# A gated-MLP block behind a long convolution: right-angle transform in four channel units, first half ordered by a list scheduler inside the kernel

## The chip, the cores and the metric

One core of one Trainium2 chip runs the kernel. The metric is the device time of one launch in microseconds (us), lower is better.

## The reference, cut to what matters

All tensors are bf16; S = 2048 rows, D = 640 channels, Fh = 864.

```python
mod = silu(c) @ w_mod                      # six vectors of 640: sa, ca, ga, sb, cb, gb
h = layernorm(x) * (1 + ca) + sa           # x = A_q
kv = conv4(A_k, shift_k) * A_v             # 4 causal taps per channel
y = irfft(rfft(kv, 2S) * rfft(ssm_k, 2S))[:S] + kv * ssm_D
x = x + ga * (h * y)
h = layernorm(x) * (1 + cb) + sb
z = gelu(h @ w_in)                         # 2048 x 1728
z1 = z[:, :864]; z2 = layernorm(z[:, 864:])
out = x + gb * ((z1 * (w_sp @ z2 + b_sp)) @ w_out)
```

The first half is everything up to the second `x`; the second half is the gated MLP.

## The kernel before, in words

**Inputs and tables of the first half.** A_k and A_v are loaded transposed (channels on partitions) by ten transposing DMAs on SP's queue (L140, L141). TensorE applies the four taps as matmuls with diagonal weights `dg` (L165), VectorE multiplies by v (L167), and the product goes to a DRAM scratch `kv_scr` (L168), from which it is read back as `XU` in the layout of the transform (L501). The transform is two steps of matmuls: step one multiplies by a cos/sin table `F1bd` (helper at L263, copied out of PSUM by ScalarE at L222 into `X1K` or `X1U`), step two by the table `M2`. M2 is made from iota, range reduction on VectorE (L181 to L189) and Sin on ScalarE (L185 to L190). `G2`, its transpose for the way back, is made by 51 TensorE transposes (L304).

**Row statistics and modulation.** The whole of x is normalised on VectorE (L356, L357) and ScalarE (L363), with a square root on ScalarE (L84). Six matrices `wm` of w_mod are loaded through two buffers and multiplied on TensorE (L380, L389), giving `gca_bf` and `gsa_bf`; GpSimd applies these to the gate `gh` (L495).

**The main loop** runs over four units of 160 channels and, in each, over 17 blocks of 128 frequencies (`kc`); blocks 0 and 16 are real, the other 15 complex. For one block of the data side TensorE forms `pu` (L244 to L252, four matmuls of 160 columns), VectorE multiplies by the kernel's transform `KH` (L416, tile `T`, 640 elements), TensorE goes back (L424, L428, eight matmuls of 160 columns into `pz`) and ScalarE copies to `Z` (L222). In the same loop TensorE and ScalarE make `KH` of the next unit (`pk`), step one of the next unit, and the way back of the unit before: TensorE transposes Z (L449, tile `pt`), VectorE copies it (L224, tile `ZT`), TensorE multiplies by `Ebd` (L459, tile `py`), and VectorE multiplies the gate (L463). Once a unit is done VectorE adds it to x (L467) and takes the statistics of the new x (L474). The third slot of KH is filled by a DMA (L286).

**The second half**: statistics and normalisation (L567, L577), TensorE transposes and their copies into `h2T` (L582, L586, L588), then four dense products on TensorE: z2 (L605), z1 (L621), w_sp times z2 (L642), and the output (L658). `w_in` (L552), `w_o` (L555) and the transposed w_sp, `wT` (L562), are loaded when the buffers of the first half are free; GpSimd multiplies w_o by gb (L557).

**What sets the order.** The kernel is written in the Tile framework: pools give buffers, semaphores follow from the tiles, and the framework's own scheduler may move instructions. Inside the main loop the author interleaves the lists of a unit by hand (`interleave`).

Of the kernel before, what the change touches and what calls it, by code (L numbers as in the profile page):

```python
# [10 lines left out]
ALU = mybir.AluOpType  # L11
# [26 lines left out]
def kernel(  # L38
# [39 lines left out]

    constp = ctx.enter_context(tc.tile_pool(name="constp", bufs=1))
# [14 lines left out]
    eps_t = constp.tile([P, 1], F32)  # L94
    nc.vector.memset(eps_t[:], EPS)
# [5 lines left out]
    ones_row = constp.tile([1, P], BF16)  # L101
    nc.vector.memset(ones_row[:], 1.0)
    zeros_bf = constp.tile([P, DU], BF16)
    nc.vector.memset(zeros_bf[:], 0.0)

    with ExitStack() as actx:
# [7 lines left out]
        gsa_bf = consta.tile([P, D], BF16)  # L114
        sk_bf = consta.tile([P, ND, 4], BF16)
        c_bf = consta.tile([P, ND], BF16)

        kpool = actx.enter_context(tc.tile_pool(name="kside", bufs=2))
        psA = actx.enter_context(tc.tile_pool(name="psA", bufs=2, space=bass.MemoryType.PSUM))
        ectx = ExitStack()  # L120
        early = ectx.enter_context(tc.tile_pool(name="early", bufs=2))
        psE = ectx.enter_context(tc.tile_pool(name="psE", bufs=2, space=bass.MemoryType.PSUM))

        nc.sync.dma_start(sk_bf[:], A_shift_k.rearrange("(t p) j -> p t j", p=P))
        ssm_fft = A_ssm_k.rearrange("(c g) (n f) -> (g n) c f", g=8, f=P)
        XK0 = kpool.tile([P, NCU, P], BF16, tag="XK")
        nc.sync.dma_start(XK0[:], ssm_fft[:, 0:NCU, :])
        d_fft = A_ssm_D.rearrange("(c g) -> g c", g=8)

        def add_D(XK, c0):  # L130
            nc.gpsimd.dma_start(out=XK[0:P:16, :, 0], in_=d_fft[:, c0:c0 + NCU], accum_op=ALU.add)

        add_D(XK0, 0)
        nc.sync.dma_start(c_bf[:], c[0].rearrange("(t p) -> p t", p=P))
        kv_in = []
        for dt in range(ND):
            kTp = early.tile([P, KPAD + S], BF16, tag="kTp", bufs=ND)
            vT = early.tile([P, S], BF16, tag="vT", bufs=ND)
            nc.gpsimd.memset(kTp[:, 0:KPAD], 0.0)
            nc.sync.dma_start_transpose(kTp[:, KPAD:], A_k[0, :, dt * P:(dt + 1) * P])  # L140
            nc.sync.dma_start_transpose(vT[:], A_v[0, :, dt * P:(dt + 1) * P])  # L141
            kv_in.append((kTp, vT))
        nc.sync.dma_start(xt[:], x_nat)
        wmv = w_mod.rearrange("(t p) (j d) -> p t j d", p=P, j=6)
        wm_tiles = []
        for j in range(6):
            wm = consta.tile([P, ND, D], BF16, tag="wm", bufs=2)
            nc.sync.dma_start(wm[:], wmv[:, :, j, :])
            wm_tiles.append(wm)

        sk = early.tile([P, ND, 4], F32, bufs=1)
        dg = early.tile([P, ND, 4, P], BF16, bufs=1)
        nc.vector.tensor_copy(sk[:], sk_bf[:])
        for dt in range(ND):
            nc.vector.tensor_tensor(dg[:, dt], ident[:, None, :].to_broadcast([P, 4, P]),
                                    sk[:, dt, :, None].to_broadcast([P, 4, P]), op=ALU.mult)
        kv_scr = dram.tile([D, S], BF16)
        SCH = 512
        for dt in range(ND):
            kTp, vT = kv_in[dt]  # L160
            for sc_i in range(S // SCH):
                ps = psE.tile([P, SCH], F32, tag="kv")
                for j in range(4):
                    o = KPAD + sc_i * SCH - j
                    nc.tensor.matmul(ps[:], lhsT=dg[:, dt, j, :], rhs=kTp[:, o:o + SCH], start=(j == 0), stop=(j == 3))  # L165
                vsl = vT[:, sc_i * SCH:(sc_i + 1) * SCH]
                nc.vector.tensor_tensor(vsl, ps[:], vsl, op=ALU.mult)  # L167
            nc.sync.dma_start(kv_scr[dt * P:(dt + 1) * P, :], vT[:])  # L168
        if "kv" in dbg:
            nc.sync.dma_start(dbg["kv"], kv_scr[:])  # L170

        cctx = ExitStack()
        cs = cctx.enter_context(tc.tile_pool(name="cscratch", bufs=2))
        TWO_PI = float(np.float32(2 * np.pi * (1 - 2.0 ** -20)))
        MAGIC = 12582912.0
        halfpi = consta.tile([P, 1], F32)
        nc.vector.memset(halfpi[:], float(np.float32(np.pi / 2 * (1 - 2.0 ** -20))))

        def sincos(dst_cos, dst_nsin, dst_sin, v, shape, tagp):
            r = cs.tile(shape, F32, tag=tagp + "r")  # L180
            nc.vector.tensor_scalar(r[:], v, MAGIC, MAGIC, op0=ALU.add, op1=ALU.subtract)  # L181
            fr = cs.tile(shape, F32, tag=tagp + "fr")
            nc.vector.tensor_tensor(fr[:], v, r[:], op=ALU.subtract)
            if dst_nsin is not None:
                nc.scalar.activation(dst_nsin, fr[:], ACT.Sin, scale=-TWO_PI)  # L185
            if dst_sin is not None:
                nc.scalar.activation(dst_sin, fr[:], ACT.Sin, scale=TWO_PI)
            if dst_cos is not None:
                nc.vector.scalar_tensor_tensor(r[:], fr[:], -1.0, fr[:], op0=ALU.mult, op1=ALU.max)  # L189
                nc.scalar.activation(dst_cos, r[:], ACT.Sin, bias=halfpi[:], scale=-TWO_PI)  # L190

        pq = cs.tile([P, 1], F32, bufs=1)
# [499 lines left out]
```

## Time and profile before

| | us |
|---|---|
| device time, median of 3 runs | 449.6 |
| lowest and highest run | 447.17, 450.35 |
| span of the profiled execution, first to last instruction | 446.3 |
| TensorE busy in it | 361.0 |
| VectorE busy | 238.1 |
| ScalarE busy | 177.2 |
| GpSimd busy | 64.5 |

The profiled execution has its span only, no time of its own; the span is 3.3 us under the median of the runs. PE is TensorE's matrix multiply, PEld its weight load, DVE VectorE, ACT ScalarE, POOL GpSimd, SPq SyncE's queue of DMA issues. A duration in the trace runs from the start to the end of one instruction; instructions of one engine that follow each other overlap a little, so the interval between two starts is shorter than the duration.

### The profile page before, as it was taken

What the parts mean: (1) busy time and instruction counts of PE and PEld (TensorE: products, weight loads), DVE (VectorE), ACT (ScalarE), POOL (GpSimd) and SP (SyncE); (2) the same over time, 40 slices, a digit from 0 to 9 for tenths busy, and PEclk for the clock granted to TensorE, in tenths of its full rate; (3) what the DMA queues carried; (4) which work ended last, traced back from release to release, by engine and by line L of the source; (5) the groups of instructions that cost most, each with busy time, mean ns of one, the idle gap of its engine ahead of it and who ended that gap; (6) DMA issues with size and microseconds to landing.
All of it is one profiled execution on the core that took longest, in us unless ns stands there. A gap on an engine that the chain in (4) does not pass through costs nothing.

```text
span 446.3 us, 6827 instructions
## 1 busy us (share of the span) xinstructions
PE 361.0 (81%) x2777; PEld 230.8 (52%) x2777; DVE 238.1 (53%) x526; ACT 177.2 (40%) x356; POOL 64.5 (14%) x68
## 2 busy tenths in 40 slices
PE   1975643684979989979552789999999999999996
PEld 0333631362967868868341455444444444445774
DVE  4779900140447777879769887640132333233553
ACT  1338888455866867823201655765200000000000
POOL 2001000799920000000100710000000000000000
PEclk9997865687999999999855799999999999999999
DMA  8999891720250050020109999500000000000222
GB/s 149 203 227 391 268 208 16 220 60 7 54 123 1 2 123 1 1 65 1 24 3 301 239 214 199 101 1 0 1 0 13 0 12 1 0 1 0 74 89 74
DMA packets 96991, 38.73 MB, mean 87 GB/s; under 512 B 86752, under 2 KB 95552, under 8 KB 96960
## 3 DMA queue, kind: packets, MB, share of 16 engines
q1 hardware_dynamic: 95424, 37.77, 34.3%
q0 software_dynamic: 1536, 0.53, 1.0%
q8 instruction: 21, 0.34, 0.3%
q14 instruction: 10, 0.08, 0.1%
HBM read 16.63 MB, written 5.24 MB: 49 GB/s over the span
## 4 chain that ended last, share of the span: by engine, by line
PE 46%; DVE 7%; DMA 2%; SPq 1%; issue 1%; ACT 0%; DVEq 0%
PE ps L642 22%; PE ps L658 7%; PE ps L621 7%; PE ps L605 6%; DMA w_in<-in_B_w_in_dram 2%; DVE T L416 2%; DVE xn L577 1%; PE pt L449 1%; DVE ZT L224 1%; PE pz L424 1%; PE py L459 1%; SPq L562 1%; DVE st L474 1%; PE pz L428 1%; PE pt L582 1%
## 5 line engine op out<-in xcount | busy, mean ns | idle before, releaser
L642 PE MATMUL ps<-wT,z 128*128 128x512 bf16 (+1 forms) x448 | 96.9, 379 | 0.0
L642 PEld LDWEIGHTS <-z 128*128 128x128 bf16 (+1 forms) x448 | 45.4, 101 | 51.3
L416 DVE TENSOR_TENSOR T<-pu,KH 128x640 bf16<-128x640 f32 x68 | 53.7, 815 | 32.4 <-PE pu L252 23.2
L645 DVE TENSOR_TENSOR gt<-ps,bsp_bc 128x512 bf16<-128x512 f32 (+1 forms) x28 | 19.3, 691 | 85.0 <-PE ps L642 85.0
L222 ACT CAST Z<-pz 128x320 bf16<-128x320 f32 x64 | 27.3, 426 | 32.5 <-PE pz L428 25.8
L424 PE MATMUL pz<-T,G 128*128 128x160 bf16 x272 | 30.4, 234 | 6.8 <-DVE T L416 6.4
L605 PE MATMUL ps<-w_in,h2T 128*128 128x432 bf16 x160 | 31.9, 351 | 0.8 <-DMA w_in<-in_B_w_in_dram 0.8
L165 PE MATMUL ps<-kTp,dg 128*128 128x512 bf16 x80 | 21.7, 413 | 13.4 <-DMA kTp<-in_A_k_dram 9.7
L638 POOL DMA_DIRECT2D bsp_bc<-in_B_b_sp_dram x4 | 2.3, 589 | 200.5 <-DVE gt L645 106.3
L658 PE MATMUL ps<-w_o,z1T 128*128 128x320 bf16 (+1 forms) x224 | 30.7, 299 | 0.0
L621 PE MATMUL ps<-h2T,w_in 128*128 128x512 bf16 (+1 forms) x140 | 30.4, 379 | 0.0
L222 ACT CAST X1K<-ps 128x512 bf16<-128x512 f32 x40 | 23.4, 586 | 14.8 <-PE ps L263 14.1
L222 ACT CAST KH<-pk 128x320 bf16<-128x320 f32 x68 | 26.9, 440 | 1.8 <-PE pk L252 0.9
L428 PE MATMUL pz<-T,G 128*128 128x160 bf16 x240 | 27.2, 234 | 0.0
L424 PEld LDWEIGHTS <-G 128*128 128x128 bf16 x272 | 20.7, 98 | 11.9 <-DVE T L416 7.0
L658 PEld LDWEIGHTS <-z1T 128*128 128x128 bf16 (+1 forms) x224 | 21.8, 97 | 8.9
L263 PE MATMUL ps<-F1bd,XU 128*128 128x256 bf16 x80 | 17.9, 300 | 8.6 <-ACT X1U L222 4.8
L495 POOL TENSOR_TENSOR gh<-gh,gca_bf 128x640 bf16<-128x640 bf16 x16 | 22.4, 1422 | 10.3 <-DVE gca_bf L393 10.3
L660 DVE TENSOR_TENSOR ot<-ps,xt 128x320 bf16<-128x320 f32 x32 | 15.7, 491 | 14.2 <-PE ps L658 14.2
L621 PEld LDWEIGHTS <-w_in 128*128 128x128 bf16 (+1 forms) x140 | 14.2, 102 | 16.0 <-issue 0.2
L611 DVE BATCH_NORM_STATS2 stz<-z 128x6 f32<-128x432 bf16 x32 | 19.4, 608 | 5.1 <-ACT z L608 4.3
L495 POOL TENSOR_TENSOR gh<-gh,gsa_bf 128x640 bf16<-128x640 bf16 x16 | 21.9, 1390 | 0.0
(132 smaller groups left out, 616.8 us busy)
## 6 DMA issues: line engine op xcount, KB each, us to landing
wm<-in_w_mod_dram SPq DMA_DIRECT2D x6, 800.0 KB, 5.4
KH<-KH SPq DMA_DIRECT2D x4, 680.0 KB, 5.5
xt<-in_A_q_dram SPq DMA_DIRECT2D x1, 2560.0 KB, 10.9
kv_scr<-vT SPq DMA_DIRECT2D x5, 512.0 KB, 10.6
XU<-kv_scr SPq DMA_DIRECT2D x4, 640.0 KB, 5.6
out_dram<-ot SPq DMA_DIRECT2D x16, 160.0 KB, 1.8
w_in<-in_B_w_in_dram SPq DMA_DIRECT2D x1, 2160.0 KB, 10.8
XKn<-in_A_ssm_k_dram SPq DMA_DIRECT2D x3, 640.0 KB, 7.7
```

The lines of the kernel that those rows point to most:

```text
L165: nc.tensor.matmul(ps[:], lhsT=dg[:, dt, j, :], rhs=kTp[:, o:o + SCH], start=(j == 0), stop=(j == 3))
L222: nc.scalar.copy(dst, src)
L416: nc.vector.tensor_tensor(T[:], pu[:, None, :, :].to_broadcast([P, 2, 2, DU]), kx, op=ALU.mult)
L424: nc.tensor.matmul(zre, lhsT=w_, rhs=x_, start=(i == 0), stop=(i == 3))
L428: nc.tensor.matmul(pz[:, 1, :], lhsT=w_, rhs=x_, start=(i == 0), stop=(i == 3))
L495: nc.gpsimd.tensor_tensor(gvu, gvu, vec[:, None, d0:d0 + DU].to_broadcast([P, GHB, DU]), op=op)
L605: nc.tensor.matmul(ps[:, :FC], lhsT=h2T[:, kt, n * P:(n + 1) * P], rhs=w_in[:, kt, Fh + fc * FC:Fh + (fc + 1) * FC], start=(kt == 0), stop ...
L611: nc.vector.bn_stats(out=stz[:, n, fc * nsubz + a, :], in_=zs[:, a, :])
L621: nc.tensor.matmul(ps[:fsz[ft], :], lhsT=w_in[:, kt, ft * P:ft * P + fsz[ft]], rhs=h2T[:, kt, sc_i * SC:(sc_i + 1) * SC], start=(kt == 0), ...
L642: nc.tensor.matmul(ps[:fsz[ft], :], lhsT=z2[:, st_i, ft * P:ft * P + fsz[ft]], rhs=wT[:, st_i, tci * TC:(tci + 1) * TC], start=(st_i == 0) ...
L645: nc.vector.tensor_tensor(gt[:fsz[ft], :], ps[:fsz[ft], :], bsp_bc[:fsz[ft], :], op=ALU.add)
L658: nc.tensor.matmul(ps[:, :HS], lhsT=z1T[:fsz[ft], ft, n * P:(n + 1) * P], rhs=w_o[:fsz[ft], ft, h * HS:(h + 1) * HS], start=(ft == 0), sto ...
```

## The change

It replaces the whole first half and reorders parts of the second.

- The transform takes frequencies 4k + 1, in 16 complex blocks in place of 17 (15 complex, 2 real). A block's forward step is 3 matmuls in place of 4 and its way back 6 in place of 8, over the same number of columns per channel (one matmul writes real and imaginary part). KH has two slots, and its DMA goes.
- The units are 128, 192, 192 and 128 channels wide; the first needs only the first 128 channels of kv.
- Every step is an entry of a `Plan` with engine, cost, tiles read and written and a due time `t`. `Plan.run` picks, again and again, the entry that can start first (ties by due time) and emits it. `manual_schedule` keeps the emitted order.
- Z is transposed by DMA from SBUF to SBUF for three units (`last_stage`, eight transposing DMAs), by TensorE for the last.
- VectorE's range reduction for M2 moves in part to GpSimd (two operations on 256 elements for each of 8 chunks); GpSimd also builds four of the five diagonals, negates parts of G2, computes 1/sqrt by a power, and adds the first three units to x. The first layer norm is applied on VectorE; copies of G2 out of PSUM go from ScalarE to VectorE.
- w_mod comes in 18 pieces of 256 or 128 columns. `gh_mod` names the whole of gca and gsa as read.
- `w_in` is loaded in two halves inside the first half. The second half normalises groups of four row tiles ahead of the products that use them; the scaling of w_o on GpSimd and the normalisation of z2 come after the first row of blocks of z1 (20 matmuls).

The core of the diff (the dense products themselves are unchanged):

```diff
+UNITS = ((0, 128), (128, 192), (320, 192), (512, 128))
+HOP = 150
+LAND = 2000
+SLOTS = dict(X=3, X1=3, KH=17, T=4, Z=2, ZT=2, wm=2, big=2, dg=2, st1=2, ga=1, s1=2, pu=3, pz=2, py=1)
...
+        while len(order) < len(ops):
+            best = None
+            for i in ready:
+                o = ops[i]
+                st = slot_time(o)
+                if st is None:
+                    continue
+                for e, cost in o["eng"].items():
+                    at = max(st, free[e])
+                    for d in o["deps"]:
+                        at = max(at, done[d] + (0 if eng_of[d] == e and e != "SP" else HOP))
+                    key = (max(at, free[e]), o["t"], i)
+                    if best is None or key < best[0]:
+                        best = (key, i, e, cost)
...
+    ctx.enter_context(tc.manual_schedule())
...
+            def turns(e):
+                e.iota(tl[v][:], [[4, KCH], [64, P]], base=4 * i * KCH + 1, channel_multiplier=0,
+                       allow_small_or_imprecise_dtypes=True)
+                e.tensor_scalar(tl[v][:], tl[v][:], pidx[:, 0:1], 1.0 / 8192.0, op0=ALU.mult, op1=ALU.mult)
+                e.tensor_scalar(tl[r][:], tl[v][:], MAGIC, MAGIC, op0=ALU.add, op1=ALU.subtract)
+            op({"POOL": 1400}, turns, w=[v, r], new=[(v, "T"), (r, "T")], t=t)
...
-                    for i, (w_, x_) in enumerate(terms):
-                        nc.tensor.matmul(zre, lhsT=w_, rhs=x_, start=(i == 0), stop=(i == 3))
+                mm(p_[:, :, 0:du], G2[:, 0, kc, :], T_[:, 0, :, 0:du], True, False)
+                mm(p_[:, :, 0:du], G2[:, 1, kc, :], T_[:, 1, :, 0:du], False, False)
+                mm(p_[:, 1, 0:du], G2[:, 2, kc, :], T_[:, 0, 0, 0:du], False, False)
...
-                        nc.tensor.transpose(pt[:, i, :], Z[:, q, :, :].rearrange("p j c -> p (j c)"), ident[:])
+                    e.dma_start_transpose(tl[ZT][:], tl[Z][:, q0:q0 + ZB, :, :].rearrange("p q j c -> p (q j c)"))
...
+            for vec, name, o in ((gca1_bf, "gca", ALU.mult), (gsa_bf, "gsa", ALU.add)):
+                op({"POOL": pool_cost(TB * du)},
+                   lambda e, vec=vec, o=o: e.tensor_tensor(gvu, gvu, vec[:, None, d0:d0 + du].to_broadcast([P, TB, du]), op=o),
+                   r=[name], w=[("gh", (u, g))], t=t)
...
-    nc.sync.dma_start(w_in[:], B_w_in.rearrange("(t p) f -> p t f", p=P))
+        get_w_in(1, 50)
+        get_w_in(0, 54)
```

SP's queue at the start of the program, before. `kTp` and `vT` are the transposed k and v of 128 channels, X the operands of the transform.

```order
L124 DMA sk_bf<-in_A_shift_k_dram 128x5x4
L127 DMA XK_105<-in_A_ssm_k_dram 128x20x128
L134 DMA c_bf<-in_c_dram 128x5x1
L140 DMA_TRANSPOSE kTp<-in_A_k_dram 128x2048
L141 DMA_TRANSPOSE vT<-in_A_v_dram 128x2048
...
L143 DMA xt<-in_A_q_dram 128x16x640
L148 DMA wm<-in_w_mod_dram 128x5x640 x2
L168 DMA kv_scr<-vT 128x2048 x5
L506 DMA XKn<-in_A_ssm_k_dram 128x20x128
L286 DMA KH<-KH 128x17x160
L501 DMA XU<-kv_scr 128x20x128
```

The same queue in the changed kernel; `big` holds k and v of 128 channels.

```order
L638 DMA sk_bf<-in_A_shift_k_dram 128x5x4
L459 DMA_TRANSPOSE big<-in_A_k_dram 128x2048
L368 DMA X<-in_A_ssm_k_dram 128x16x128
L461 DMA_TRANSPOSE big<-in_A_v_dram 128x2048
L459 DMA_TRANSPOSE big<-in_A_k_dram 128x2048
L494 DMA xt<-in_A_q_dram 128x8x640
L488 DMA kv_scr<-big 128x2048
L461 DMA_TRANSPOSE big<-in_A_v_dram 128x2048
L368 DMA X<-kv_scr 128x16x128
```

The first read-back from kv_scr moved from behind all five stores and a DMA of KH to behind one store.

GpSimd around the modulation of the gate, before: 32 operations in one series, nothing of the main loop among them.

```order
L216 IOTA v_398 128x128
L131 DMA XKn<-in_A_ssm_D_dram 8x20x1 x2
L495 TENSOR_TENSOR gh<-gh,gca_bf 128x4x160 x2
L495 TENSOR_TENSOR gh<-gh,gsa_bf 128x4x160 x2
...
L131 DMA XKn<-in_A_ssm_D_dram 8x20x1
```

GpSimd in the changed kernel from the last diagonal on; G is G2, xt is x.

```order
L470 TENSOR_TENSOR dg<-ident,sk 128x512
L358 TENSOR_SCALAR G_88<-G_88 128x1024
L194 TENSOR_SCALAR rstd_101<-mv_100 128x8
L195 TENSOR_TENSOR rstd_101<-rstd_101,mhalf 128x8
L458 MEMSET big 128x16
L565 TENSOR_TENSOR gh<-gh,gca_bf 128x4x128 x2
...
L565 TENSOR_TENSOR gh<-gh,gsa_bf 128x4x192
L630 TENSOR_TENSOR xt<-xt,gh 128x4x128 x4
L565 TENSOR_TENSOR gh<-gh,gca_bf 128x4x192
...
L630 TENSOR_TENSOR xt<-xt,gh 128x4x192 x4
```

The same 32 operations now alternate by unit with 12 additions to x that VectorE had.

VectorE in the changed kernel at the end of the second unit (`T` of 768 elements), where the last pieces of gca and gsa are made.

```order
L546 SCALAR_TENSOR_TENSOR gca_bf<-s_1388,ga 128x128
L426 TENSOR_TENSOR T<-pu,KH 128x768
L551 TENSOR_TENSOR gsa_bf<-s_1416,ga 128x128
L426 TENSOR_TENSOR T<-pu,KH 128x768
L485 TENSOR_TENSOR big<-s_1446,big 128x512
...
L592 TENSOR_TENSOR gh<-gh,py 128x16x32 x4
L374 TENSOR_TENSOR X<-X,D_col 128x16
L426 TENSOR_TENSOR T<-pu,KH 128x768 x5
L633 BN_STATS st_72<-xt 128x6 x4
```

In the kernel before gca and gsa stand ahead of the first T of the loop; here they stand between the last T of the second unit, and the first four multiplications of the gate follow five operations later.

## Rows read from the trace of the kernel before

**Rows 1.** The page, span in 40 slices: busy tenths, granted TensorE clock in tenths.

```profile
PE   1975643684979989979552789999999999999996
DVE  4779900140447777879769887640132333233553
...
PEclk9997865687999999999855799999999999999999
```

**Rows 2.** Six stretches: length; PE, PEld, DVE, ACT, POOL busy us (instructions); clock, DMA share, GB/s.

```profile
0.00:94.25 94.25, 52.79 (x329) 30.88 (x330) 46.36 (x154) 54.69 (x106) 20.61 (x34) 0.78 0.78 199
94.25:135.87 41.62, 31.87 (x356) 26.50 (x354) 16.80 (x22) 27.58 (x59) 31.50 (x24) 0.92 0.30 65
135.87:197.89 62.02, 55.63 (x724) 49.09 (x722) 47.77 (x87) 43.45 (x100) 0.00 (x0) 1.00 0.15 35
...
220.40:233.60 13.20, 8.00 (x84) 6.20 (x82) 6.89 (x10) 0.42 (x1) 0.74 (x2) 0.50 0.11 20
233.60:261.85 28.25, 14.38 (x113) 9.35 (x114) 25.11 (x67) 11.18 (x18) 10.00 (x7) 0.71 1.04 254
261.85:446.30 184.45, 180.89 (x941) 93.78 (x938) 73.41 (x147) 33.52 (x58) 1.12 (x2) 1.00 0.18 41
```

**Rows 3.** Timeline of the first 171 us, chosen rows: start, length, engine, operation, idle before.

```profile
9.66 8.02 PE L165 MATMUL ps<-kTp,dg 128*128 128x512 bf16 x24 [9.66 <-DMA kTp<-in_A_k_dram]
...
61.93 12.27 ACT L363 ACTIVATE gh<-xt,nmr,rstd 128x640 bf16<-128x640 bf16 x15
...
80.30 0.82 DVE L393 SCALAR_TENSOR_TENSOR gca_bf<-modbc 128x640 bf16<-128x640 f32 x1 [20.19 <-ACT modbc L385]
...
94.25 1.56 DVE L416 TENSOR_TENSOR T<-pu,KH 128x640 bf16<-128x640 f32 x2 [6.65 <-PE pu L250]
...
166.80 3.01 DVE L416 TENSOR_TENSOR T<-pu,KH 128x640 bf16<-128x640 f32 x4
```

**Rows 4.** Groups by line and shape, whole span: count, busy us, mean ns, idle before.

```profile
L416 DVE TENSOR_TENSOR T<-pu,KH 128x640 bf16<-128x640 f32 x68 | 53.7, 815 | 32.4 <-PE pu L252 23.2 <-PE pu L250 6.6 <-ACT X1U_next L222 1.5
...
L222 ACT CAST Z<-pz 128x320 bf16<-128x320 f32 x64 | 27.3, 426 | 32.5 <-PE pz L428 25.8 <-PE pz L424 5.9
...
L222 ACT CAST X1K<-ps 128x512 bf16<-128x512 f32 x40 | 23.4, 586 | 14.8 <-PE ps L263 14.1
L495 POOL TENSOR_TENSOR gh<-gh,gca_bf 128x640 bf16<-128x640 bf16 x16 | 22.4, 1422 | 10.3 <-DVE gca_bf L393 10.3
...
L167 DVE TENSOR_TENSOR vT<-ps,vT 128x512 bf16<-128x512 f32 x20 | 13.7, 687 | 8.2 <-DMA vT<-in_A_v_dram 7.3 <-PE ps L165 0.9
...
L467 DVE TENSOR_TENSOR xt<-xt,gh 128x2560 bf16<-128x2560 bf16 x4 | 6.0, 1488 | 0.1
...
L216 POOL IOTA v<- 128x256 f32 x8 | 3.4, 482 | 26.4 <-DVE fr L183 26.4
...
L567 DVE BATCH_NORM_AGGREGATE mv<-st 128x2 f32<-128x24 f32 x16 | 2.1, 205 | 0.0
```

**Rows 5.** TensorE's groups from 135.87 to 197.89 us, the first and the last.

```profile
L424 PE MATMUL pz<-T,G 128*128 128x160 bf16 x136 | 15.1, 232 | 1.5 <-DVE T L416 1.3
...
L459 PE MATMUL py<-Ebd,ZT 128*128 128x64 bf16 x72 | 3.9, 193 | 1.3 <-DVE ZT L224 1.3
```

**Rows 6.** DMA issues by tile: KB each, median us from issue to landing.

```profile
kv_scr<-vT SPq DMA_DIRECT2D x5, 512.0 KB, 10.6
XU<-kv_scr SPq DMA_DIRECT2D x4, 640.0 KB, 5.6
```

**Rows 7.** Timeline from 235 to 258 us, VectorE and GpSimd.

```profile
235.13 3.72 DVE L474 BATCH_NORM_STATS2 st<-xt 128x6 f32<-128x160 bf16 x16
...
241.71 2.23 DVE L577 TENSOR_SCALAR xn<-xt,mv,rstd 128x640 bf16<-128x640 bf16 x6
...
247.99 10.00 POOL L557 TENSOR_TENSOR w_o<-w_o,gb_bf 128x640 bf16<-128x640 bf16 x7 [26.85 <-DMA w_o<-in_B_w_out_dram]
...
252.81 3.93 DVE L577 TENSOR_SCALAR xn<-xt,mv,rstd 128x640 bf16<-128x640 bf16 x3
```

More of the change, by code (lines that the diff above doesn't have):

```diff
@@ L135 @@
[L135 to L156, printed above, removed]
@@ new lines, in mm, with pe, act_cost, dve_cost @@
+        def mm(o, w, x, start, stop):
+            nc.tensor.matmul(o, lhsT=w, rhs=x, start=start, stop=stop)
+        def pe(*cols):
+            return {"PE": sum(max(c, 100) for c in cols) / 2.2}
+        def act_cost(n):
+            return 170 + 0.85 * n
+        def dve_cost(n):
+            return 150 + 1.04 * n
+        def fast_cost(n):
+            return 130 + 0.55 * n
+        def pool_cost(n):
+            return 120 + 2.3 * n
+        def dma(kb, rate):
+            return {"SP": 50 + kb * 1024 / rate}
@@ new lines @@
+        load_x(0, -6)
+        load_x(1, -3)
+        for n in range(NT):
+            ln1(n, 3 + n * 0.7)
+        for n in range(NT):
+            xn(n, 14 + n * 0.3)
+        for w in range(len(WS)):
+            for i, j in enumerate((2, 1, 0)):
+                mod(j, w, 6 + w * 3 + i)
+        for i, (j, w) in enumerate([(j, w) for j in (3, 4, 5) for w in range(len(WS))]):
+            mod(j, w, 36 + 1.5 * i)
+        for u in range(NU):
+            t = t_of[u]
+            for g in range(NT // TB):
+                gh_mod(u, g, t + (16 if u == 0 else 8) + g)
+            t = t_of[u + 1]
+            if u < NU - 1:
+                last_stage(u, t + 3)
+            else:
+                last_stage_pe(u, t + 3)
+            for g in range(NT // TB):
+                resid(u, g, t + 12 + g)
@@ new lines, with prep, norm @@
+    xns = {}
+    def prep(g):
+        n0, n1 = g * TB, (g + 1) * TB
+        for n in range(n0, n1):
+            nc.vector.bn_aggr(out=mv2[:, n, :], in_=st2[:, n, :, :])
+        rstd_from_var(rstd2[:, n0:n1], mv2[:, n0:n1, 1])
+    def norm(g):
+        for n in range(g * TB, (g + 1) * TB):
+            xns[n] = bwork.tile([P, D], BF16, tag="xn2", bufs=2 * TB, name="xn")
+            nc.vector.tensor_scalar(xns[n][:], xt[:, n, :], mv2[:, n, 0:1], rstd2[:, n:n + 1],
+                                    op0=ALU.subtract, op1=ALU.mult)
@@ L607, with call @@
             zsl = z2[:, n, fc * FC:(fc + 1) * FC]
             nc.scalar.activation(zsl, ps[:, :FC], ACT.Gelu_apprx_tanh)
-            zs = zsl.rearrange("p (a b) -> p a b", a=nsubz)
-            for a in range(nsubz):
-                nc.vector.bn_stats(out=stz[:, n, fc * nsubz + a, :], in_=zs[:, a, :])
+            nc.vector.bn_stats(out=stz[:, n, fc, :], in_=zsl)
+    def call(f, *a):
+        return lambda: f(*a)
+    NG = NT // TB
+    prep(0)
+    prep(1)
+    norm(0)
+    for dt in range(ND):
+        flip(0, dt)
@@ L613 @@
+    norm(1)
+    prep(2)
+    prep(3)
+    for g in range(NG):
+        flips = [call(flip, g + 1, dt) for dt in range(ND)] if g + 1 < NG else []
+        for i in range(TB):
+            z2_tile(g * TB + i)
+            for f in flips[2 * i:2 * i + 2]:
+                f()
+        if g + 2 < NG:
+            norm(g + 2)
     z1T = bpool.tile([P, NFT, S], BF16)
-    if dbg and fsz[-1] < P:
-        nc.vector.memset(z1T[fsz[-1]:, NFT - 1, :], 0.0)
-    SC = 512
     for ft in range(NFT):
-        for sc_i in range(S // SC):
-            ps = psB.tile([P, SC], F32, tag="mm", bufs=4)
+        for sc_i in range(S // TC):
+            ps = psB.tile([P, TC], F32, tag="mm", bufs=5, name="ps")
```

960 lines of the change are left out of this document (500 added, 460 removed).

## The prediction

> **What bounds the kernel now.** I read the slices of the page first. TensorE is solid from the 24th slice on and has holes in the first 23; its granted clock is below full in most of slices 4 to 10 and again in 20 to 23 [rows 1]. No engine is full over the first half either, so what costs time there is order, not work. The busy times by stretch say how much [rows 2]: before the main loop, 94.25 us in which TensorE is busy 52.8, VectorE 46.4, ScalarE 54.7; a first unit of 41.6 us; two units in 62.0 us; a way back of the last unit in 13.2 us at half clock; 28.25 us in which the second half starts; and 184.45 us in which TensorE is busy 180.9. That last stretch is TensorE's own work and the change adds or removes no product there, so it stays. The timeline shows the pattern of the start: ScalarE normalises x for 12.3 us in one run, VectorE sits idle 20.2 us before gca, and the first product T of the loop starts only at 94.25 [rows 3].
>
> **The change part by part.**
>
> *Start until the first T of unit 0.* The transform's first unit now needs one fifth of kv. On SP's queue the read-back stands behind one store and no longer behind five and a DMA of KH. The first k lets TensorE start at 9.66 us [rows 3], and one small load less stands ahead of it now, so this is no later. The chain that then ends last is the table M2. GpSimd makes 8 chunks; one is an iota of 0.48 us and two operations on 256 elements. GpSimd's arithmetic with a constant is in no row; its products take 1422/640 = 2.2 ns per element [rows 4], so I take 0.57 us per operation; the ends are the iota's 0.48 below and, above, 1.42, a whole product of 640. A chunk is then 1.6 us, 1.9 with the wait between dependent operations, 15 in all; 8 us of other GpSimd work (iotas, a diagonal, the spread silu) stand among them, so the last is ready at some 23 us, the sixth at 18. On ScalarE, in its order, behind the sixth chunk's sines come 8 copies of step one at 0.586, the last sines, 16 copies of KH at 0.37 (0.426 for 320 elements and 0.586 for 512 give 0.83 ns per element [rows 4]) and 8 more copies: 20 + 4.7 + 1.8 + 6.0 + 4.7 = 37. The store and the read-back would be there at 36 even at the medians of 10.6 and 5.6 us [rows 6], counted from the convolution's end at about 20. I take 38 for the first T. With 1.42 per operation it is 13 more, 51.
>
> *The main loop with everything laid into it.* The order lists 1202 matmuls from there to the end of the first half; their columns add up to 239,000, which at 2.4 GHz are 99.6 us: 47.4 until the last piece of gsa, 52.2 behind it. For how dense the loop can be I take the two steady units of before: 724 matmuls in 62.02 us at full clock [rows 2], namely 512 of 160 columns, 68 of 256, 72 of 128 and 72 of 64 (first and last of the groups in [rows 5]), 113,152 columns or 47.1 us, a share of 76%. The changed loop has longer matmuls and none that transposes Z behind a copy in three of four units, but layer norm, modulation and three fifths of the convolution come in. I take 78%: 99.6 / 0.78 = 128 us. The others lie below: VectorE has 64 products T (four in 3.01 us at 640 elements [rows 3] is 0.73 each; by 1.0 ns per element, from 687 at 512 to 815 at 640 [rows 4], 0.61 for 512 and 0.86 for 768, together 47), 20 gate products and 12 of the convolution at 0.6 (19), 64 statistics at 0.23 [rows 7] (15), and some 15 of layer norm: 96. ScalarE has 64 copies of Z, 48 of KH and 64 of step one: 27 + 21 + 38 = 86. These three are what must overlap, and before they did so at three quarters.
>
> *The way back of the last unit.* Before, 13.2 us for five blocks in strict turn [rows 2]. Now four blocks, with copies alternating between two engines and three buffers; their columns are in the sum above. I add 4.
>
> *From the last gate product to the end.* Before it is 446.3 - 233.6 = 212.7 us. Now: 20 statistics at 0.23 (4.7), four additions of 512 elements at 1.488/2560 per element (1.2 [rows 4], 1.4 with their gaps), 8 aggregations at 2.1/16 (1.0 [rows 4]), one over the root on GpSimd (in no row; 1.0, at least two sequential operations, ends 0.3 and 3), four normalised tiles at 0.37 (1.5 [rows 7]), five blocks of transposes with copies (3): 12.6. Behind that the dense part: 184.45, plus the 113 matmuls that before ran ahead of it [rows 2], 32 of 432 columns (5.8) and of its 80 transposes the 60 not already counted (3.3): 193.5. Together 206, and 1 for a clock that starts at half: 207. So this part brings 6 us and no more, although w_in is there early: the wait for it before ran beside statistics and transposes.
>
> *Covered.* The DMA transposes of Z cost nothing while SP's queue stays ahead; without that cover a unit's gate products come later, which TensorE fills with the next unit. KH's DMA and VectorE's copy of ZT lay beside TensorE already. The conversion of the layer norm from ScalarE to VectorE is in VectorE's 96.
>
> *Sum.* 38 + 128 + 4 + 207 = 377 us of span. The median of the runs is 3.3 over the span of the profiled execution, so 380 us against 449.6, 15% less.
>
> [...] VectorE normalises six tiles in 2.23 us while GpSimd is free, 0.37 each, and three in 3.93, 1.3 each, while GpSimd scales w_o [rows 7]. [...] By the row, at most 9 first-half tiles, two fast gate products and some additions may run beside GpSimd in the loop, 0.9 each, 14 us of VectorE at worst, which leaves it at 110 of 128: no change of the sum, but a reason for the upper part of the range. T itself, with one operand in PSUM, is 0.815 in the mean over the whole span, though GpSimd was busy for 31.5 us of its loop [rows 2, 4].
>
> **The rivals.**
>
> *GpSimd's series becomes the end.* gh_mod waits for the last piece of gca and gsa, so none of its 32 operations can start before the end of unit 1; with the 12 additions to x they are 28,672 elements at 2.2 ns, 63.7 us, in one series that the last gate products wait for. [...]
>
> *The start is late.* If the constant operations on GpSimd cost 1.42 and a store lands later than 10.6 us, the loop starts at 51 to 60: 393 to 402.
>
> *The list is tighter than the old order.* At 90% of TensorE's columns the loop ends with GpSimd: 38 + 53 + 64 + 5 + 207 + 3.3 = 370; with a start at 32 it is 364.
>
> *The clock stays low: slower.* With holes in its work TensorE ran at a mean of 0.78 before the loop and at 0.50 in the way back [rows 2]. If the loop leaves such holes, each column there takes twice its time. 99.6 us of columns all at 1.2 GHz, at the same 78%, make 255 in place of 128 and 507 in all; the loss eats the 70 us gained once the lower level holds 55% of the loop. Against it: the steady units were granted 1.00 throughout at 76% columns, and the changed loop has no long wait for one engine. [...]
>
> **How the numbers follow.** Forecast, 365 to 392: 0.68. GpSimd's series or a late start, 392 to 412: 0.17. Tighter, 352 to 365: 0.09. Low clock or another loss of 70 us: 0.05. A list that by chance of stalls ends where the old order did: 0.01. The range 358 to 408 leaves out the two outer ends. About 1% is what a measurement of this kernel tells from no change; by that bound faster has 0.94, the same 0.01, slower 0.05.
>
> **What would show it.** The first T near 38 us; the last gate product near 170; TensorE at full clock from about 40; the last stretch solid, some 194 us, behind a gap of about 12; GpSimd solid from about 100 to 165. Wrong would be: T starting beyond 55 us with VectorE waiting for GpSimd; GpSimd full and TensorE idle at the end of the first half; a clock below 0.8 between 60 and 160; or the dense part longer than 200 us.

## The result, and the profile after

The changed kernel takes 380.19 us (median of 4 runs, 379.7 to 381.42) against 449.89 us for the kernel before (4 runs): a ratio of 0.847, 95% interval 0.8445 to 0.8502. The prediction said 380. The sum came out; two of its terms did not, and they cancelled by luck.

First the slices of the page, as in [rows 1]:

```profile
PE   1388699899999999821999999999999999999996
DVE  7769899566737988897777669012333233234553
POOL 8942320583829579062200078000000000000000
PEclk9999999999999999985799999999999999999999
```

TensorE is nearly solid from the 6th slice on but for slices 18 and 19, the way from the first half to the second; before it had holes up to the 23rd. GpSimd (POOL) is busy in most slices of the first half, but nowhere solid for long. The stretches, with cuts at the first product T (L426), the last T and the first product with w_in (L758); the columns are those of [rows 2]:

```profile
0.00:43.80 43.80, 24.58 (x149) 13.50 (x150) 33.97 (x98) 23.44 (x53) 26.34 (x45) 1.00 0.90 192
43.80:156.50 112.70, 105.87 (x1099) 82.73 (x1099) 85.90 (x165) 79.82 (x185) 59.96 (x47) 1.00 0.81 166
156.50:181.40 24.90, 8.38 (x117) 6.68 (x115) 19.46 (x61) 5.80 (x10) 9.23 (x8) 0.70 0.31 65
181.40:377.70 196.30, 192.30 (x1035) 100.80 (x1032) 89.31 (x178) 41.76 (x71) 18.27 (x17) 0.99 0.26 58
```

| stretch, us of span | before | after | gain |
|---|---|---|---|
| start to the first T | 94.25 | 43.8 | 50.5 |
| first T to the last gate product's end | 139.35 | 124.9 | 14.5 |
| last gate product to the end | 212.7 | 209.0 | 3.7 |
| span | 446.3 | 377.7 | 68.6 |

(After, the last gate product ends at 168.7.) By these cuts 50.5 of the 68.6 us lie before the loop. Work has crossed the cut, though: the matmuls ahead of the first T cover 81,650 columns before and 39,424 after, and the modulation and more than half of layer norm and convolution now stand inside the loop; loop and last way back are 14.5 us shorter all the same. In the loop TensorE is busy 105.87 of 112.70 us, at full clock. The chain that ended last shows that the dense part is TensorE's own work, as before:

```profile
207.79 9.12 PE ps L758 x50
216.91 30.22 PE ps L790 x140
247.13 96.69 PE ps L809 x448
343.82 30.57 PE ps L821 x224
...
374.42 0.49 DVE ot L823
```

With the first 26.4 us of the products with w_in (from 181.4 on) this is one stretch of 196.3 us; before it was 184.45 us, behind 113 matmuls that ran ahead of it [rows 2].

What sets the first T is seen in chosen rows of the timeline, VectorE and TensorE alternating:

```profile
37.57 1.68 POOL L195 TENSOR_TENSOR rstd<-rstd,mhalf 128x8 f32<-128x8 f32 x1
39.28 1.16 DVE L510 TENSOR_SCALAR gh<-xt,mv,rstd 128x640 bf16<-128x640 bf16 x3 [2.17 <-POOL rstd L195]
40.35 0.68 DVE L355 COPY G<-s 128x1024 bf16<-128x1024 bf16 x1
40.95 2.23 DVE L510 TENSOR_SCALAR gh<-xt,mv,rstd 128x640 bf16<-128x640 bf16 x4
41.09 1.02 PE L231 MATMUL s<-big,dg 128*128 128x512 bf16 x4 [1.43 <-DVE G L355]
42.40 0.83 PE L231 MATMUL pu<-X,M 128*128 128x256 bf16 x9
43.10 0.68 DVE L355 COPY G<-s 128x1024 bf16<-128x1024 bf16 x1
43.70 0.25 DVE L374 TENSOR_TENSOR X<-X,D_col 128x24 bf16<-128x24 bf16 x1
43.80 1.87 DVE L426 TENSOR_TENSOR T<-pu,KH 128x512 bf16<-128x512 f32 x3
```

VectorE stands in its order before a normalisation that waits 2.17 us for GpSimd's power. Behind it is the copy of G, for that copy's PSUM buffer TensorE waits, and behind TensorE's wait stands the first `pu`. That `pu` is not the last to come: from 39.28 on VectorE has no idle time, and T starts right behind four more normalised tiles, a copy of G and the addition to X. So the first T hangs on VectorE's series, with those 2.17 us of waiting ahead of it.

### The profile page after: what moved, and what is told of

The parts are those of the page before. It is cut to its first block, busy times and chain, and to the rows that moved or that the text cites. A ratio compares the mean times of both kernels' runs of the same rounds, so it can differ in the third digit from the quotient of the medians.

```text
span 377.7 us, 6095 instructions
## 1 busy us (share of the span) xinstructions
PE 331.1 (88%) x2394; PEld 203.7 (54%) x2394; DVE 228.6 (61%) x497; ACT 150.8 (40%) x318; POOL 113.8 (30%) x117
## 3 DMA queue, kind: packets, MB, share of 16 engines
q1 hardware_dynamic: 111184, 39.18, 48.8%
## 4 chain that ended last, share of the span: by engine, by line
PE 56%; DMA 3%; DVE 3%; issue 3%; POOL 1%; ACT 1%; ACTq 0%; DVEq 0%; POOLq 0%
PE ps L809 26%; PE ps L821 8%; PE ps L790 8%; PE ps L758 7%; PE pz L231 3%; DMA ZT<-Z 2%; PE pu L231 2%; PE tp L746 1%; DVE xn L740 1%; DMA wm<-in_w_mod_dram 1%; PE s L231 1%; POOL xt L630 1%; DVE st L633 1%; DVE T L426 1%; PE py L231 0%
## 5 line engine op out<-in xcount | busy, mean ns | idle before, releaser
L809 PE MATMUL ps<-wT,z 128*128 128x512 bf16 (+1 forms) x448 | 96.9, 379 | 0.0
L809 PEld LDWEIGHTS <-z 128*128 128x128 bf16 (+1 forms) x448 | 45.4, 101 | 51.3
L426 DVE TENSOR_TENSOR T<-pu,KH 128x512 bf16<-128x512 f32 (+1 forms) x64 | 50.6, 817 | 16.5 <-PE pu L231 9.2
L231 PE MATMUL pu<-X,M 128*128 128x128 bf16 (+3 forms) x384 | 49.8, 254 | 0.7 <-ACT KH L415 0.7
L231 PE MATMUL pz<-T,G 128*128 128x192 bf16 (+3 forms) x384 | 45.4, 255 | 3.1 <-DVE T L426 2.8
L393 ACT CAST X<-s 128x512 bf16<-128x512 f32 x80 | 43.9, 592 | 6.6 <-PE s L231 5.8
L231 PEld LDWEIGHTS <-M 128*128 128x128 bf16 x384 | 33.1, 97 | 9.3 <-issue 1.5
L443 ACT CAST Z<-pz 128x256 bf16<-128x256 f32 (+1 forms) x64 | 27.2, 428 | 23.8 <-PE pz L231 22.2
L231 PE MATMUL s<-F1bd,X 128*128 128x256 bf16 x160 | 29.6, 277 | 5.0 <-ACT X L393 2.8
L758 PE MATMUL ps<-big,h2T 128*128 128x432 bf16 x160 | 31.9, 354 | 0.0
L821 PE MATMUL ps<-w_o,z1T 128*128 128x320 bf16 (+1 forms) x224 | 30.7, 299 | 0.0
L790 PE MATMUL ps<-h2T,big 128*128 128x512 bf16 (+1 forms) x140 | 30.4, 379 | 0.0
L415 ACT CAST KH<-pu 128x256 bf16<-128x256 f32 (+1 forms) x64 | 25.7, 432 | 11.6 <-PE pu L231 9.9
L821 PEld LDWEIGHTS <-z1T 128*128 128x128 bf16 (+1 forms) x224 | 21.8, 97 | 8.9
L565 POOL TENSOR_TENSOR gh<-gh,gsa_bf 128x512 bf16<-128x512 bf16 (+1 forms) x16 | 22.3, 1396 | 9.0 <-DVE gsa_bf L551 8.0
L565 POOL TENSOR_TENSOR gh<-gh,gca_bf 128x512 bf16<-128x512 bf16 (+1 forms) x16 | 22.3, 1396 | 4.6 <-DVE gca_bf L546 4.6
```

The lines of the kernel that those rows point to most:

```text
L231: nc.tensor.matmul(o, lhsT=w, rhs=x, start=start, stop=stop)
L393: e.copy(dst, tl[name][:].rearrange("p i (j g) -> p i j g", g=8))
L415: op({"ACT": act_cost(2 * du)}, lambda e: e.copy(tl[KH][:, :, 0:du], tl[pk][:, :, 0:du]), r=[pk], w=[KH], t=t)
L426: e.tensor_tensor(T_[:, :, :, 0:du], tl[pu][:, :, None, 0:du].to_broadcast([P, 2, 2, du]), tl[KH][:, None, :, 0:du].to_broadcast([P, 2, 2, ...
L443: op({"ACT": act_cost(2 * du)}, lambda e: e.copy(tl[Z][:, 0:du // 4, 2 * kc:2 * kc + 2, :], tl[pz][:, :, 0:du] .rearrange("p r (q c) -> p ...
L565: lambda e, vec=vec, o=o: e.tensor_tensor(gvu, gvu, vec[:, None, d0:d0 + du].to_broadcast([P, TB, du]), op=o),
```

## The experiments

Twelve kernels, each compared with the kernel before in the same runs. First T, last T, first product with w_in and span are read from one trace of each, in us:

| run | time | ratio to before | first T | last T | w_in | span |
|---|---|---|---|---|---|---|
| changed kernel | 380.2 | 0.8445 to 0.8502 | 43.8 | 156.5 | 181.4 | 377.7 |
| a_due | 411.9 | 0.9154 to 0.9249 | 57.1 | 188.2 | 212.7 | 409.7 |
| a_free | 394.1 | 0.8736 to 0.8836 | 48.8 | 174.5 | 196.4 | 392.5 |
| a_lateread | 399.7 | 0.8878 to 0.8955 | 84.7 | 176.9 | 199.7 | 396.6 |
| a_all | 471.0 | 1.045 to 1.0562 | 122.0 | 248.3 | 272.4 | 468.9 |
| a_lnlate | 383.5 | 0.852 to 0.8613 | 42.0 | 161.4 | 184.4 | 380.4 |
| a_m2dve | 383.4 | 0.8505 to 0.8591 | 46.2 | 158.9 | 183.6 | 381.1 |
| a_split | 380.2 | 0.8405 to 0.8507 | 45.0 | 158.2 | 182.0 | 378.6 |
| a_peflip | 386.4 | 0.8524 to 0.8668 | 45.6 | 168.4 | 188.4 | 384.8 |
| a_winlate | 378.8 | 0.8359 to 0.8499 | 43.8 | 157.5 | 180.4 | 377.0 |
| a_res2dve | 378.5 | 0.8376 to 0.849 | 43.5 | 156.1 | 179.7 | 376.5 |
| a_tail | 385.6 | 0.855 to 0.8629 | 45.3 | 158.0 | 175.6 | 384.8 |
| a_best2 | 385.6 | 0.8559 to 0.8636 | 44.9 | 156.8 | 174.4 | 383.8 |

### Is it the order? a_due, a_free, a_lateread, a_all

```diff
-key = (max(at, free[e]), o["t"], i)     # a_due
+key = (o["t"], max(at, free[e]), i)
-ctx.enter_context(tc.manual_schedule())     # a_free
-load_X("XU%d" % u, ..., [("kvs", dt) for dt in dts])     # a_lateread
+load_X("XU%d" % u, ..., [("kvs", dt) for dt in range(ND)])
```

**a_due**: 

> The changed kernel with one rule turned round: the list scheduler takes, of what is ready, the entry with the earliest due time and only then the one that can start first. The operations stay the same 100%, so this separates order from form. Theory (the gain is order): engines that work in order now stand behind entries that were due but could not start yet; the first product T comes later than the 43.8 us of the changed kernel and the loop is less dense than 88%, 390 to 430 us. Rival (the gain is the new forms of the transform, and any sensible order would do): 379 to 384 us, first T within 2 us of 43.8.

Measured 411.9: the theory. The start loses 13.3 us and the loop 18.4, with the same operations.

**a_free**: 

> The changed kernel without the line that keeps the emitted order, so the framework's own scheduler may move instructions, as in the kernel before. Theory (order): the scheduler does not know the due times, so work that nobody waits for gets ahead of the chain to the first T; first T at 50 to 70 us, 388 to 420 us in all. Rival (the list alone does it, the framework leaves its order nearly as it is): 379 to 384 us.

Measured 394.1: the theory in the total. But the first T comes at 48.8, earlier than expected, 5.0 us behind the changed kernel; the loop loses 13.0 us (125.7 in place of 112.7), and 3 come back behind it.

**a_lateread**: 

> The changed kernel with one edge added: the read-back of kv for the first unit waits for all five stores, as in the kernel before, not for its own fifth. Theory (the first T hangs on the early read-back, and the time before it is only half used): first T at 55 to 65 us, the loop shorter by what has been done ahead of it (four fifths of the convolution, modulation, layer norm, some 8 us), in all 386 to 394 us. Rival (the start is set by GpSimd's table and the read-back is hidden): 379 to 383 us.

Measured 399.7, more than either, and the first T at 84.7, far later than expected. Its stretches:

```profile
0.00:84.70 84.70, 47.13 (x252) 23.91 (x253) 56.26 (x149) 24.51 (x57) 58.31 (x72) 0.81 0.89 202
84.70:176.90 92.20, 90.11 (x1022) 75.96 (x1020) 68.26 (x114) 76.48 (x182) 27.91 (x21) 0.99 0.56 111
```

The first T is 40.9 us later and the last only 20.4: half of the wait was filled with work taken out of the loop, which is now 92.2 us with TensorE busy 90.11 of them. So the early read-back is worth some 20 us in this list, and the first T by itself overstates what a start costs.

**a_all** (a_due, a_lateread and the Z of a_peflip below): 

> The changed kernel with three steps undone at once: earliest due time first, the first read-back behind all five stores, and Z of all units transposed by TensorE. Alone they cost 32, 19 and 6 us. Theory (each is a part of its own of the gain): 380 + 57 = 437 us, 430 to 442, which would account for most of the 69 us. Rival (the first two hit the same wait before the loop, so that the larger hides the smaller): 410 to 425 us, and the rest of the gain lies in something that no run has touched.

Measured 471.0, 91 us over the changed kernel and 22 over the kernel before. Both were wrong: the losses neither add nor overlap, they make each other worse. The timeline before the first T, TensorE's rows and two of GpSimd's, shows how:

```profile
54.83 2.07 PE L231 MATMUL pu<-X,M 128*128 128x256 bf16 x21
67.96 1.23 PE L231 MATMUL s<-wm,sc_rep 128*128 128x256 bf16 x5 [11.06 <-DMA wm<-in_w_mod_dram]
...
87.81 0.44 PE L231 MATMUL s<-wm,sc_rep 128*128 128x128 bf16 x5 [0.88 <-DVE big L485]
101.29 1.15 POOL L565 TENSOR_TENSOR gh<-gh,gsa_bf 128x512 bf16<-128x512 bf16 x1
102.39 1.04 POOL L470 TENSOR_TENSOR dg<-ident,sk 128x512 bf16<-128x512 bf16 x1
103.49 5.72 PE L231 MATMUL s<-big,dg 128*128 128x512 bf16 x16 [15.25 <-POOL dg L470]
115.78 1.04 PE L231 MATMUL s<-F1bd,X 128*128 128x256 bf16 x4 [6.57 <-DMA X<-kv_scr]
```

With all five stores now ahead of the first T, everything that the due times put among them stands on that path: a modulation whose matrix is not yet loaded (11.06 us), and the diagonal of the last taps, a 1.04 us operation on GpSimd that stands there behind eight modulations of the gate, and for which TensorE waits 15.25 us. So the new operations in a poor order are slower than the old kernel, and by a_due another rule for the order, alone, loses 32 of the 69 us. That the whole gain is the order's is not shown: the old operations in the new order were not run. What the new forms took off TensorE can be counted in the traces. Up to the first product with w_in its matmuls cover 279,600 columns; before they cover 298,400, without the 33 products with w_in and the 60 transposes that now come later. That is 7.8 us at 2.4 columns per ns, an estimate from the rows of L809 and L821 above, both at a granted clock of 1.00: 448 matmuls of 512 columns take 216 ns each, 224 of 320 columns 136, so 192 columns more take some 80 ns. What the work moved between the other engines is worth was tested for two parts only (a_m2dve, a_res2dve).

### Is it the form? a_split, a_peflip

a_split cuts the matmuls, for example (lines left out between them)

```diff
-mm(pu[:, :, 0:du], M2[:, 0, kc, :], x[:, 2 * kc:2 * kc + 2, 0:du], True, False)
...
+mm(pu[:, 0, 0:du], M2[:, 0, kc, :], xr, True, False)
...
+mm(pu[:, 1, 0:du], M2[:, 0, kc, :], xi, False, True)
```

> The changed kernel with its matmuls cut to one unit's width, as in the kernel before: four in place of three in a forward block, eight in place of six on the way back, over the same columns; 256 matmuls more. Theory (TensorE's time goes by columns; in the kernel before, four matmuls of 160 columns started 69 ns apart, 66.7 of them columns at 2.4 GHz): 256 x 2 to 10 ns, +0.5 to +2.5 us, 380 to 383. Rival (the longer matmuls are where the loop got denser, since the sum of matmul durations fell by 48 us from the kernel before): +10 us or more.

Measured 380.2, loop 113.2 us against 112.7: the theory's lower end, no difference that can be measured. TensorE's time here goes by columns; the lower sum of matmul durations is no gain, since matmuls that follow each other overlap: those of L809 last 379 ns each, and 448 of them take 96.69 us, 216 ns each.

a_peflip calls the last unit's way back for all units:

```diff
-            if u < NU - 1:
-                last_stage(u, t + 3)
-            else:
-                last_stage_pe(u, t + 3)
+            last_stage_pe(u, t + 3)
```

> The changed kernel with Z of all four units transposed by TensorE, as in the kernel before, in place of DMA for three of them: 128 transposes of 128 columns more (16,384 columns, 6.8 us at 2.4 GHz) and 16 copies out of PSUM. Theory (the loop is 88% columns, so TensorE's added work shows nearly in full): 384 to 390 us. Rival (the DMA's 8 us landing at the end of the loop cost as much, and with it the wait of 1.0 us that held up later work): 378 to 382 us.

Measured 386.4, +6.2 us: the theory, at nearly the whole price of its 6.8 us of columns. But it is a sum of opposite parts: the first T comes 1.8 us later, the loop is 10.1 us longer, and the way from the last T to the first product with w_in is 4.9 us shorter. On that way the changed kernel has the last transposing DMA of the third unit, and it stands in the chain that ended last:

```profile
149.71 8.03 DMA ZT<-Z
...
157.79 0.41 PE py L231 x8
```

TensorE's transposes for the third unit alone, which might keep the 4.9 us without most of the 10.1, were not run.

### What sets the start? a_lnlate, a_m2dve

```diff
-op({"DVE": 1150}, stats, r=xs, w=[("mv1", n)], ...)     # a_lnlate; the first product writes "go"
+op({"DVE": 1150}, stats, r=xs + ["go"], w=[("mv1", n)], ...)
```

> The changed kernel with the row statistics of x (16 entries on VectorE, and what follows from them) held back until the first product T is emitted. In the changed kernel VectorE reached x's normalisation at 39.3 us and waited 2.2 us for GpSimd's power, and the first step of the data side stood behind that. Theory (the start can be cut, the loop takes the work at no cost since TensorE's columns set it): first T at 40 to 42, the whole 376 to 379 us. Rival (work moved out of the start comes back in the loop one to one): 379 to 382. Second rival (the gate products then wait for the normalised x): the last gate product later than 170 us and 385 to 395.

Measured 383.5: the start as the theory said (42.0), the total as none of the three did: 1.8 us won before the loop, 6.7 lost in it (119.4 us), 1.9 won behind it. The chain of waits shows why:

```profile
50.20 0.65 DVE T L426
50.85 0.80 DVE st L501 x2
...
51.68 0.21 DVE mv L502
51.88 0.76 DVE st L501 x2
...
52.70 0.09 issue
52.79 0.65 DVE T L426
```

The statistics now stand between the products T, and TensorE waits for T, 7.5 us over the span and 2.8 in the changed kernel. The last gate product ends at 172.5, later than 170 as the second rival had it, but not for its reason: it stands 11.1 us behind the last T, 12.2 in the changed kernel. The products T were late, and the gate product with them.

a_m2dve moves the two constant operations of a chunk, and the costs that the list counts with them:

```diff
 def turns(e):
-    e.tensor_scalar(tl[v][:], tl[v][:], pidx[:, 0:1], 1.0 / 8192.0, ...)
-    e.tensor_scalar(tl[r][:], tl[v][:], MAGIC, MAGIC, ...)
 def angles(e):
+    e.tensor_scalar(tl[v][:], tl[v][:], pidx[:, 0:1], 1.0 / 8192.0, ...)
+    e.tensor_scalar(tl[r][:], tl[v][:], MAGIC, MAGIC, ...)
```

> The changed kernel with the two constant operations of each of the 8 chunks of the table M2 moved from GpSimd (0.5 to 1.3 and 1.1 us) to VectorE (0.4 to 0.5 us by its two operations of the same size). Theory of the prediction (GpSimd's chain of chunks sets the start): the last chunk, done at 24.8 us, comes 8 us or more earlier and the first T 4 to 8 us earlier than 43.8, 372 to 377 us. Rival (the table is ready long before its use, and the first T hangs on the engines' in-order work between 30 and 43 us): first T within 2 us of 43.8, 379 to 384 us with the 7 us that VectorE has more.

Measured 383.4, first T at 46.2: the rival, a little above its 2 us. GpSimd was relieved of 13.2 us before the first T (26.34 to 13.13 us busy) and VectorE loaded with 3.3, and the start grew by 2.4. But the table came no sooner, so the run does not test an early table. VectorE finished the last chunk's angles at 24.9 us, against 25.7 in the changed kernel, and ScalarE's last sines start later. The changed kernel's row comes first:

```profile
27.30 0.50 ACT L338 ACTIVATE M<-T,halfpi 128x256 bf16<-128x256 f32 x1
```

```profile
28.95 0.50 ACT L338 ACTIVATE M<-T,halfpi 128x256 bf16<-128x256 f32 x1
```

What speaks against GpSimd's table as the limit is the changed kernel's own trace: ScalarE is busy without a gap from 22.72 us to the end of the last sines at 27.80, so those waited for ScalarE's copies of step one and not for GpSimd.

### What sets the way into the dense part? a_winlate, a_res2dve, a_tail, a_best2

```diff
+nc.gpsimd.tensor_copy(w_in[h][:, 0, 0:8], gh[:, NT - 1, D - 8:D])     # a_winlate
+nc.sync.dma_start(w_in[h][:], ...)     # both now behind the first half's list
...
-op(eng, lambda e: e.tensor_tensor(sl, sl, gh[...], op=ALU.add), ...)     # a_res2dve
+op(eng, lambda e: (nc.vector if u >= 2 else e).tensor_tensor(sl, sl, gh[...], op=ALU.add), ...)
```

**a_winlate**: 

> The changed kernel with w_in loaded at the end of the first half, as in the kernel before: each of its two halves is requested only after the last gate product. (Eight columns of the buffer are written first, by GpSimd, only to make the load wait.) Theory of the prediction (its load ran beside statistics and transposes and cost nothing): 379 to 383 us. Rival (the early load is what shortened the way from the last gate product to the dense part): the first product with w_in starts 5 to 12 us later than at 181.4, 385 to 393 us.

Measured 378.8 (2 runs): the prediction's theory. Requested only after the last gate product, at 169.0 us, and landing 7.5 us later (median), w_in is still there before the first product at 180.4.

**a_res2dve**: 

> The changed kernel with the four additions to x of unit 2 (768 elements each) on VectorE in place of GpSimd, in the same place of the order. Theory (the end of the first half hangs on GpSimd, which takes 6.6 us for these four behind a late gate product, and VectorE's statistics queue behind them): VectorE takes 0.6 us each, the last gate product and the first normalised tile come 3 to 5 us earlier, 375 to 378 us. Rival (VectorE is the series there anyway, or the wait for the transposing DMA of Z is): 379 to 382 us.

Measured 378.5; the first product with w_in comes 1.7 us earlier, less than the theory said, and the total cannot be told from the changed kernel's. One row of each timeline, the changed kernel first, tells of a second effect:

```profile
162.25 1.44 DVE L588 TENSOR_TENSOR gh<-gh,wm 128x512 bf16<-128x512 bf16 x1 [0.16 <-ACT wm L586]
```

```profile
160.92 0.42 DVE L588 TENSOR_TENSOR gh<-gh,wm 128x512 bf16<-128x512 bf16 x1
```

The same product takes 1.44 us while GpSimd adds (160.17 to 166.76) and 0.42 when GpSimd rests, 1.0 us apart on this row.

**a_tail** is a_res2dve with the second half's opening rewritten (the transposes of the second group also start one row tile later):

```diff
-for n in range(g * TB, (g + 1) * TB):     # statistics of units 2 and 3
+for n in range(g * TB, (g + 1) * TB) if u < 2 or g == 0 else ():
...
-prep(0)
-prep(1)
 norm(0)
...
+prep(1)     # with the missing statistics of its group
 norm(1)
...
+    prep(g + 2)
     norm(g + 2)
```

> The changed kernel with unit 2's additions on VectorE (378.5 us by itself) and, behind the last gate product, only the first group of four row tiles taken through its statistics before the normalised tiles; the other 24 statistics and 12 aggregations come behind the first normalised group, beside TensorE's first dense products. Theory (VectorE is one solid series from 158 us to the first normalised tile at 176.8, so TensorE waits for just what stands in that series): the series is 24 x 0.25 + 4 x 0.14 = 6.5 us shorter, first product with w_in at 174 to 176, 372 to 375 us. Rival (the wait moves to the second group's transposes, for which VectorE is then late): first product as early, but a hole of 3 to 6 us behind the first group, 376 to 380 us.

The first product came at 175.6, 5.8 us earlier, as the theory said; then the rival came, dearer than it was priced:

```profile
181.49 1.99 PE L767 MATMUL ps<-big,h2T 128*128 128x432 bf16 x10
...
190.33 1.01 POOL L197 TENSOR_TENSOR rstd<-rstd,mhalf 128x4 f32<-128x4 f32 x1
191.38 1.52 DVE L749 TENSOR_SCALAR xn<-xt,mv,rstd 128x640 bf16<-128x640 bf16 x4 [1.41 <-POOL rstd L197]
191.88 1.78 PE L755 MATMUL tp<-ident,xn 128*128 128x128 bf16 x8 [3.42 <-DVE xn L749]
193.46 3.01 PE L767 MATMUL ps<-big,h2T 128*128 128x432 bf16 x10
```

VectorE prepares the third group only when it is due, TensorE runs dry for 3.42 us, and ten products take 1.99 us before that hole and 3.01 behind it. From 181.4 to 215.8 us the granted clock is 0.85 in the mean, over the same stretch of the changed kernel 0.97. From the first product to the end it is 209.2 us in place of 196.3; of the 12.9 us more, TensorE is idle for 7.8 and busy for 5.1.

**a_best2**:

```diff
-op({"POOL": 1400}, turns, ...)
+op({"POOL": 2100}, turns, ...)
```

> The kernel of the run before with one number more changed: a chunk of the table M2 on GpSimd is entered in the list scheduler at 2100 in place of 1400 (its three operations take 1.9 to 2.7 us). Theory (the scheduler set VectorE's normalisation of x ahead of work it could have done, since it believed GpSimd to be done sooner; with a true cost it would not): first T 1 to 2 us earlier, 1 to 3 us under the run before. Rival (a greedy list answers to any number with another order, better or worse): within 4 us on either side, the first T unmoved.

Measured the same 385.6: the rival, with the first T at 44.9 in place of 45.3. No run beat the changed kernel by more than its measurement is uncertain.

## Why the prediction was right, and where it was not

- **Start, 38 forecast, 43.8 measured (+5.8).** The step that failed is the chain: it added up ScalarE's copies without a wait for TensorE, and put 1 us for all that comes behind them. A chunk of the table took 1.9 to 2.7 us where 1.6 was priced (its constant operations take 0.5 to 1.3 and 1.1 us, between the ends used), and the last was done at 24.8 us where 23 was forecast. ScalarE's copies of step one, for which the chain gave 37, end at 40.3: 3.3 of the 5.8 us. On that way, behind the last sines, ScalarE waits 3.4 us for TensorE's matmuls. The other 2.5 are VectorE's: busy 34 of the 43.8 us, it waited for GpSimd's power, and four normalised tiles stood in its order ahead of T. In a_lnlate these are gone, the copies end at 39.9, and the first T comes 1.8 us earlier.
- **Loop and last way back, 128 + 4 forecast, 112.7 + 12.2 measured (-7.1).** The mis-sized term is the density, 78% of columns, taken from two old units at 76%. The 2.4 GHz at which its columns are counted is in no trace as a frequency; the runs show in its place the 2.4 columns per ns above. Behind the last T some 4.3 us of the 99.6 us of columns are left (10,240: three blocks of 1024, 48 of 64, 32 of 128), so the loop held 95.3 in 112.7, 85%. a_split shows that longer matmuls are not the reason; a_free, with the same operations in another order, has a loop of 125.7 us, and a_due one of 131.1. So density goes with the order of the list, and the rate read from the old order was no limit for the new operations. This was the rival "tighter than the old order", with a late start on top. The last way back was undersized: 12.2 us where 4 and its columns (4.3) were allowed; TensorE waits 2.8 us there for a gate product on VectorE, 1.1 for ScalarE's copies of `py` and 1.0 for the last transposing DMA of Z.
- **GpSimd's series.** The claim that gh_mod waits for the last gca and gsa piece was false. The scheduler enters a whole vector as read, but that only shapes the order; on the chip an operation waits for the pieces that it reads. The lines for L565 show it: the first operation starts at 72.6 us, behind a wait for the first piece of gca (4.6 us), and a second wait is for the second piece of gsa (8.0). The last pieces of gca and gsa come only behind the start of 12 of the 32 operations. The rows of the two last pieces stand first:

```profile
96.01 0.29 DVE L546 SCALAR_TENSOR_TENSOR gca_bf<-s,ga 128x128 bf16<-128x128 f32 x1 [0.66 <-PE s L231]
97.42 0.29 DVE L551 TENSOR_TENSOR gsa_bf<-s,ga 128x128 bf16<-128x128 f32 x1 [0.20 <-PE s L231]
```

```profile
L565 POOL TENSOR_TENSOR gh<-gh,gca_bf x16: 1147/1396/1643, 72.6 to 148.2; 128x512 bf16<-128x512 bf16 x8, 128x768 bf16<-128x768 bf16 x8
L565 POOLq EVENT_SEMAPHORE  x2: 17/17/17, 74.4 to 91.2; - x2
...
  DVE gsa_bf L551: 8.0, 1
  DVE gca_bf L546: 4.6, 1
```

  The price of 2.2 ns per element was right (1147 ns for 512, 1643 for 768). The rival, and the "GpSimd solid from 100 to 165" that was to show a step right, rested on a wait that isn't there.
- **Last gate product to the end, 207 forecast, 209.0 measured.** The dense part measured 196.3 (193.5 and 1 forecast), the way there 12.7 (12.6). That w_in's early load brings nothing was right by a_winlate. The part brought 3.7 us where 6 were forecast.
- **Z by DMA.** Costing it at nothing was right up to the last T, where TensorE has no wait for it. Behind the last T it was not quite nothing: the third unit's last DMA is 8.03 us of the chain that ended last. What it saves in all, 6.2 us by a_peflip, stood in the columns.
- **Low clock.** The loop ran at 1.00, and in the eleven experiments read by stretch at 0.95 (a_free) or more, so the rival did not come true. Ahead of the first T the granted clock was 0.69 in a_all, with TensorE busy for 52.9 of 122.0 us, and 0.82 in a_due (25.7 of 57.1), but 1.00 in the changed kernel (24.6 of 43.8). In a_all, the one run slower than the kernel before, the waits weigh more than the clock: TensorE is idle for 69 of the 122 us before the first T.

The errors of +5.8, -7.1 and +2.0 cancelled, so the total was better than its parts: that it came out within 0.2 us is luck. What the prediction got right is where the gain is, in the first half with the dense products untouched, and that order is a large part of it (32 us by a_due). What stays open is how the 69 us divide between single rules of the list, the new forms and the work moved between engines: a_all shows that the parts do not add.

## What to carry to other kernels

Time to a stage's first instruction is a poor measure of a start when idle engines can take work out of that stage: half of a_lateread's 40.9 us came back. A density read from the old kernel holds for the old order; bound it above by the engine's own columns too, not only by the rate seen. And before pricing a wait, check whether it stands on the chip or only in a planner's table.

## What the runs showed that was not expected

- Executions with the same order of instructions in the start were granted different clocks there: between 20 and 30 us 1.00 in the changed kernel, 0.87 in a_res2dve, 0.76 in a_tail, with the first T at 43.8, 43.5 and 45.3. In a_winlate it was 0.86, with the first T at 43.8 as well. What decides it is not in the trace.
- GpSimd's one-over-root is no small thing at the end of a chain: 1.0 to 1.2 us for 128x4, 1.68 for 128x8 and 2.9 for 128x16 in the changed kernel, the last of which held VectorE up for 3.3 us.
